# Key-feature sums as two column tiles, output weights in ten pieces, and a new instruction list

## The chip, the cores and the metric

The kernel runs on one core of a Trainium2 chip. The metric is the device time of one execution in microseconds; the median of three runs of the kernel before is 293.02 us. TensorE is the matrix engine (PE in the profile, with PEld for its weight loads), VectorE is DVE, ScalarE is ACT, GpSimd is POOL, and SyncE is SP, which here only issues DMAs.

## The reference

Two attention layers over the same input x (2048 tokens, 640 features, 32 heads of 20) are mixed by a gate per token. Cut to what matters:

```python
g = sigmoid((x * gate_w).sum(-1, keepdims=True))
# layer A: linear attention with softmax features
q, k, v = split(x @ wqkv)                       # 32 heads of 20
phi(t) = concat[softmax(t @ w_phi), softmax(-(t @ w_phi))]
kv  = sum over tokens of phi(k)^T v             # per head 40 x 20
z   = sum over tokens of phi(k)
a   = (phi(q) @ kv) / (phi(q) @ z + 1e-6) @ wo_A
# layer B: four segments of 512 tokens
p   = softmax(q k^T * scale + causal mask)      # inside a segment
mem = (pq @ M) / (pq @ z + 1e-6)                # memory of earlier segments
b   = (sig(beta) * mem + (1 - sig(beta)) * p v) @ wo_B;  M += pk^T v;  z += sum pk
out = g * a + (1 - g) * b
```

## The kernel before, in words

All matmul inputs are bf16 and sums are f32 in PSUM. Tokens are cut into 16 chunks of 128, and the 640 features into five chunks of 128. The program is one long list of words, `ORDER`. Each word is a step of a kind of work, such as `X0`, with a number behind it for the PSUM bank, or `a` where ACT and not DVE takes the copy out of PSUM. The words are run in order, and each engine keeps its instructions in that order, so the list alone decides what stands behind what on every engine. The kinds that matter here:

- `T`: x of the first 512 tokens turned on TensorE (4 x 5 transposes). `L`: the other three quarters of x, by a transposing DMA on SP. `F` and `W`: the feature matrix w_phi multiplied into the key and query weights; `F` needs the transposed key weights, which a DMA brings.
- `k`, `v`, `q`: keys, values and queries of layer B (5 matmuls each into a bank; `k1`, `v1`, `q1` the copies; `k2`, `q2` the DMAs on SP that lay keys and queries out for the scores). `K`, `Y`: key and query features of layer B.
- `A`: key features of layer A for a token chunk. `A0` is 10 matmuls, `A1` and `A2` two exps on ACT, `A3` to `A5` the sum, the reciprocal and the product on DVE, which goes to `phk`. `B`: the values `vA`, and the gate's sum.
- `S` and `s`: the sums z of the features. `X`: the sums kv. Ten `X0` (five chunks of features, two signs) have 16 matmuls each, one for every token chunk, and accumulate in one bank; `X1` is the masked copy to `KV` on DVE.
- `P`: attention scores. `P0` writes four banks (`st_ps`, from the fourth on a single buffer) with four row tiles of 32 rows, `P1` is one exp of 128 x 2048 on ACT, `P3` the mask on POOL. There are 80 such steps. `U`: scores times values on four column tiles of 32 columns (`uv_ps`), `U1` the copy to `uT`, `U2` a transposing DMA, `U3` to `U5` the division. `V`: the same for the last four heads' groups without tiles.
- `f`: query features of layer A (exps `f1`, `f2`). `d`: their denominators, `d0` 40 small matmuls and `d1` to `d6` a chain on DVE. `n`: numerators, `n0` and `n1` three matmuls each, `n2` and `n3` the scaling on DVE (which needs `d6`), `n4` the addition on POOL.
- `M`: the memory of layer B. `R`: the end of layer A's buffers; `R0` also loads the output weights `WoA` and `WoB` by two DMAs of 800 KB on SP. `l`: transposing DMAs of the finished rows. `o`: output projections, `o0` 10 matmuls. `t`, `b`, `p`, `a`, `e`, `z`, `h`: the same for the last 512 tokens, in parts.

In `products` (the word `X0`) features `c * 128` to `c * 128 + 127` belong to seven or eight heads, `lo` to `hi`; so each matmul has 128 stationary columns and (hi - lo) x 20 = 140 or 160 moving ones, and the mask `hm` keeps of the result only the blocks in which feature and value are of the same head.

Of the kernel before, what the change touches and what calls it, by code (L numbers as in the profile page):

```python
# [15 lines left out]
def kernel(  # L16
# [367 lines left out]
    def products(n, step, at, ev):  # L384
        t = item("X", n)
        c, sgn = divmod(n, 2)
        lo, hi = min(w[1] for w in ROWS if w[0] == c), max(w[2] for w in ROWS if w[0] == c)
        if step == 0:
            t.ps = bank([P, hi - lo, DH], "kv_ps", at)
            for sc in range(NCH):  # L390
                ten.matmul(t.ps, lhsT=phk[:, sc, c * P:(c + 1) * P, sgn],
                           rhs=vA[:, sc, lo * DH:hi * DH],
                           start=(sc == 0), stop=(sc == NCH - 1))
        else:
            vec.tensor_tensor(out=KV[:, c, sgn, lo - 6 * c:hi - 6 * c], in0=t.ps,
                              in1=hm[:, c, lo - 6 * c:hi - 6 * c, None].to_broadcast([P, hi - lo, DH]),
                              op=ALU.mult)
# [4 lines left out]
    def second_half(n, step, at, ev):  # L402
# [8 lines left out]
        wO = ctx.enter_context(tc.tile_pool(name="wO", bufs=1))  # L411
        lt.WoA = wO.tile([P, KC, D], BF16, name="WoA")
        lt.WoB = wO.tile([P, KC, D], BF16, name="WoB")
        syn.dma_start(out=lt.WoA, in_=rows5(A_wo))
        syn.dma_start(out=lt.WoB, in_=rows5(B_wo))

    def reorder(n, step, at, ev):
        c = 2 * n + step
# [398 lines left out]
    def tail_out(j, step, at, ev):  # L817
# [5 lines left out]
        else:  # L823
# [2 lines left out]

    STEPS = dict(w=lambda n, step, at, ev: warm_up(4, 2), T=turned, A=key, B=value, F=fold("F", WkA, WkT), W=fold("W", WqA, WqT), I=masks,
                 J=beta_gate, G=token_gate, O=both_gates, S=sums, s=blocks, X=products, Z=clear, R=second_half,
                 r=reorder, L=load_x, D=load_q, k=keys, K=key_features, v=values, q=queries, f=features,
                 d=weights, n=numerators, Y=query_features, P=scores, V=attended, U=attended_cols, M=memory, l=rows,  # L830
                 o=outputs, t=tail_A, b=tail_B, h=tail_out,
                 p=tail_first, a=tail_mid, e=tail_next, z=tail_last)
# [3 lines left out]


    ORDER = (
# [60 lines left out]

    done = {}  # L900
    for word in "".join(ORDER).split():
        i = done.get(word[:2], 0)
        done[word[:2]] = i + 1
# [33 lines left out]
```

## Time and profile before

| | |
|---|---|
| median of 3 runs | 293.02 us (291.64 to 293.09) |
| profiled execution, its own time | 292.36 us |
| its span, first to last instruction | 290.6 us |
| PE, DVE, ACT, POOL busy | 96%, 83%, 82%, 63% of the span |
| granted TensorE clock | 1.00 throughout |
| HBM | 5.61 MB read, 2.62 MB written |

The busy share of an engine is an average over stages. The profile names all instructions by one line, 117 (a helper records them), so the tiles tell them apart: `kv_ps` is X, `st_ps` P, `uv_ps` U, `num_ps` n, `o_ps` o and the tail, `k_ps` A, `v_ps` B, `proj` k and v, `fold_ps` F and W. The first transposed weights lie in the tile `phk`, which is free at that time.

### The profile page before, as it was taken

What the parts mean: (1) busy time and instruction counts of PE and PEld (TensorE: products, weight loads), DVE (VectorE), ACT (ScalarE), POOL (GpSimd) and SP (SyncE); (2) the same over time, 40 slices, a digit from 0 to 9 for tenths busy, and PEclk for the clock granted to TensorE, in tenths of its full rate; (3) what the DMA queues carried; (4) which work ended last, traced back from release to release, by engine and by line L of the source; (5) the groups of instructions that cost most, each with busy time, mean ns of one, the idle gap of its engine ahead of it and who ended that gap; (6) DMA issues with size and microseconds to landing.
All of it is one profiled execution on the core that took longest, in us unless ns stands there. A gap on an engine that the chain in (4) does not pass through costs nothing.

```text
span 290.6 us, 8207 instructions
## 1 busy us (share of the span) xinstructions
PE 278.1 (96%) x3233; PEld 176.2 (61%) x3233; DVE 239.8 (83%) x576; ACT 239.6 (82%) x260; POOL 183.8 (63%) x305
## 2 busy tenths in 40 slices
PE   8999999999999999999999999999999999898994
PEld 4676666667677546565546556556555555566673
DVE  5969999999699539999889988798898769989613
ACT  2478976998867899999999988999899998888801
POOL 8050000037346846797996899989789996998610
PEclk9999999999999999999999999999999999999999
DMA  7999960100110694546243425141736114356422
GB/s 226 252 237 215 166 142 11 36 2 20 20 20 20 203 158 89 72 86 134 39 92 72 106 58 104 39 106 36 124 72 139 26 41 111 83 122 126 106 62 90
DMA packets 79591, 28.10 MB, mean 97 GB/s; under 512 B 69952, under 2 KB 79552, under 8 KB 79552
## 3 DMA queue, kind: packets, MB, share of 16 engines
q1 hardware_dynamic: 78608, 26.84, 45.3%
q10 hardware_dynamic: 944, 0.74, 0.8%
q8 instruction: 25, 0.41, 0.6%
q14 instruction: 14, 0.11, 0.1%
HBM read 5.61 MB, written 2.62 MB: 28 GB/s over the span
## 4 chain that ended last, share of the span: by engine, by line
PE 66%; ACT 18%; DMA 5%; DVE 4%; POOL 3%; issue 3%; DVEq 0%; ACTq 0%; SPq 0%; POOLq 0%
ACT PT L117 15%; PE o_ps L117 9%; PE proj L117 8%; PE v_ps L117 8%; PE k_ps L117 8%; PE st_ps L117 7%; PE pf_ps L117 6%; PE q_ps L117 6%; PE uv_ps L117 4%; PE kv_ps L117 4%; DMA phk<-in_A_wqkv_dram 3%; PE mem_ps L117 2%; PE num_ps L117 2%; ACT ET L117 2%; PE zb_ps L117 1%
## 5 line engine op out<-in xcount | busy, mean ns | idle before, releaser
L117 ACT ACTIVATE PT<-st_ps 128x2048 bf16<-128x2048 f32 (+1 forms) x83 | 151.2, 1826 | 18.5 <-PE st_ps L117 14.0
L117 POOL TENSOR_SCALAR_AFFINE_SELECT PT<-PT 128x512 bf16<-128x512 bf16 (+2 forms) x116 | 80.5, 708 | 37.7 <-ACT PT L117 37.2
L117 PEld LDWEIGHTS <-xT 128*128 128x128 bf16 x640 | 59.5, 98 | 28.4 <-issue 5.7
L117 PE MATMUL st_ps<-qTp,kTs 32*128 32x384 bf16 (+3 forms) x512 | 31.8, 300 | 5.0 <-ACT PT L117 4.7
L117 ACT ACTIVATE Ek<-k_ps 128x640 bf16<-128x640 f32 x32 | 26.2, 893 | 6.2 <-PE k_ps L117 4.3
L117 POOL TENSOR_TENSOR Msb<-Msb,mtmp 128x84 f32<-128x84 f32 x24 | 9.3, 386 | 33.9 <-DVE mtmp L117 33.7
L117 DVE TENSOR_TENSOR t<-num_ps,dd 128x320 f32<-128x320 f32 x64 | 28.0, 481 | 2.3 <-POOL oA L117 1.3
L117 POOL TENSOR_TENSOR oA<-t,t 128x320 bf16<-128x320 f32 x32 | 29.1, 914 | 0.9 <-DVE t L117 0.7
L117 PEld LDWEIGHTS <-oT 128*128 128x128 bf16 x240 | 22.2, 98 | 10.4 <-issue 2.2
L117 PEld LDWEIGHTS <-kTs 32*128 32x128 bf16 (+1 forms) x552 | 14.8, 92 | 20.3 <-issue 16.3
L117 PE MATMUL proj<-WvB,xT 128*128 128x320 bf16 x160 | 26.2, 300 | 0.2 <-ACT vB L117 0.2
L117 PE MATMUL proj<-WkB,xT 128*128 128x320 bf16 x160 | 25.9, 300 | 0.0
L117 PE MATMUL q_ps<-xT,WqB 128*128 128x512 bf16 x100 | 24.9, 380 | 0.0
L117 PE MATMUL pf_ps<-xT,WqA 128*128 128x512 bf16 x100 | 24.9, 379 | 0.0
L117 PE MATMUL v_ps<-WvA,xT 128*128 128x320 bf16 (+1 forms) x160 | 24.5, 300 | 0.0
L117 PE MATMUL k_ps<-qTp,xT 128*128 128x320 bf16 x160 | 23.7, 299 | 0.1
L117 DVE TENSOR_REDUCE ksum<-Ek 128x64 f32<-128x1280 bf16 x16 | 23.3, 1455 | 0.0
L117 ACT ACTIVATE ET<-pf_ps 128x512 bf16<-128x512 f32 x40 | 22.0, 627 | 0.0
L117 POOL TENSOR_TENSOR oB<-td,tm 128x320 bf16<-128x320 f32 (+4 forms) x25 | 20.8, 835 | 0.4
L117 PE MATMUL o_ps<-WoA,oT 128*128 128x320 bf16 x120 | 20.3, 300 | 0.3 <-DVE tm L117 0.3
L117 PE MATMUL uv_ps<-PT,vB 128*32 128x512 bf16 (+1 forms) x448 | 20.4, 302 | 0.1
L117 PEld LDWEIGHTS <-phk 128*128 128x128 bf16 x370 | 17.6, 98 | 4.4 <-DMA phk<-in_A_x_dram 1.7
(115 smaller groups left out, 490.0 us busy)
## 6 DMA issues: line engine op xcount, KB each, us to landing
out_dram<-osb SPq DMA_DIRECT2D x12, 160.0 KB
qTp<-qd SPq DMA_DIRECT2D x8, 128.0 KB
WvB<-in_B_wv_dram SPq DMA_DIRECT2D x1, 800.0 KB
vA<-in_B_wq_dram SPq DMA_DIRECT2D x1, 800.0 KB
WvA<-in_A_wqkv_dram SPq DMA_DIRECT2D x1, 800.0 KB
WoA<-in_A_wo_dram SPq DMA_DIRECT2D x1, 800.0 KB
WoB<-in_B_wo_dram SPq DMA_DIRECT2D x1, 800.0 KB
qTp<-qd SPq DMA_DIRECT2D x8, 96.0 KB
```

Of the source, the lines that this page charges most:

```text
L117: return lambda *a, **k: kept(f(*a, **k))
```

## The change

1. In `products`, each matmul of 128 stationary columns becomes two of 64, set on the left and the right half of the array by `tile_position`. The first token chunk still multiplies all 140 or 160 value columns, so that the whole bank is written; the 15 others multiply only the 80 columns of the four heads that the 64 features touch. 160 matmuls become 320.
2. `R0` no longer loads the output weights. A new word `c0`, ten times in the list, loads one chunk of 128 rows (160 KB) each, on SP.
3. `ORDER` is written anew, with 1609 words instead of 1599 (the ten `c0`). A few copies go from one engine to the other: of `v1` three more on ACT, of `U1` and `o1` three each more on DVE; in the tail ACT takes four `h0` instead of an `h0` and an `h1`.

```diff
             for sc in range(NCH):
-                ten.matmul(t.ps, lhsT=phk[:, sc, c * P:(c + 1) * P, sgn],
-                           rhs=vA[:, sc, lo * DH:hi * DH],
-                           start=(sc == 0), stop=(sc == NCH - 1))
+                for f in range(c * P, (c + 1) * P, 64):
+                    a, b = (lo, hi) if sc == 0 else (f // DH, -(-(f + 64) // DH))
+                    r = f - c * P
+                    ten.matmul(t.ps[r:r + 64, a - lo:b - lo, :], lhsT=phk[:, sc, f:f + 64, sgn],
+                               rhs=vA[:, sc, a * DH:b * DH], start=(sc == 0), stop=(sc == NCH - 1),
+                               tile_position=(0, r), skip_group_check=True)
...
-        syn.dma_start(out=lt.WoA, in_=rows5(A_wo))
-        syn.dma_start(out=lt.WoB, in_=rows5(B_wo))
+    def load_o(n, step, at, ev):
+        W, w = ((lt.WoA, A_wo), (lt.WoB, B_wo))[n // KC]
+        syn.dma_start(out=W[:, n % KC, :], in_=rows5(w)[:, n % KC, :])
```

The places of the list that the prediction speaks of: the start, the first X blocks, the last denominators with their numerators, and the end.

```diff
-        "T00 w0 T1 T01 T02 T1 T1 T03 k00 T1 k01 k1 k02 I0 k03 k1 k00 k1 k1 K0 k01 K1 k1 K0 k02 K2 "
-        "K1 v03 k1 K2 K0 k00 k1 v1a K1 v01 k1 K2 F00 K0 L0 F01 K1 v1 v02 F1a K2 F2a v03 F1 F2 v1a "
+        "T00 w0 T1 k01 T02 k1 T03 T1 T1 k00 T01 k1 k02 T1 k03 k1 k00 K0 K1 k1 k01 K2 k1 K0 k02 I0 "
+        "v03 K1 v00 k1 k1 v1a v01 K0 K2 K1 v02 v1a v1 K2 F00 F01 v1 k2 F1a k03 F1 F2a F2 F00 k1 "
...
-        "s0 X00 s0 P1 U1 s0 U2 X02 s0 X1 s0 s0 s0 P3 P00 s0 X01 P1 X1 X03 s0 X1 s0 s0 s0 U3 P3 "
+        "B03 U3 s0 U4 M6 B12 s0 U5 B2 s0 U01 M7 B3 B4 s0 P3 P00 U1 X00 P1 s0 U2 s0 X03 s0 X1 s0 "
+        "s0 X02 X1 s0 P3 s0 P00 k01 P1 X1 k00 s0 k1 k03 s0 k1 s0 P3 K0 K1 P00 X02 P1 U01 s0 k1 U3 "
...
-        "U2 P1 Y2 o00 d1 M5 P3 P00 l0 M01 o1a M4 P1 d2 o00 M2 d3 M3 d4 U3 d5 U4 U5 o2 P00 o1a d6 "
-        "n02 P1 n13 P3 n00 n2 n3 n12 n2 M5 U03 n3 Y0 Y1 P00 n4 U1 o00 P1 M4 U2 P3 Y2 n4 n02 n13 "
+        "U03 o1 M5 d02 U1 U4 U2 U5 P00 d1 M00 P1 P3 o01 M2 M03 d2 l0 M3 o1 P3 P00 o02 M2 P1 U3 d3 "
+        "U4 M4 M3 n01 d4 M5 n10 o1 o2 P00 d5 o02 P3 P1 M4 d6 U5 n2 U03 l0 n3 o1a P3 P00 U1 n01 P1 "
...
-        "p02 V1 p11 V2 V3 P3 P00 o00 P1 M5 a0 M4 b0 o1a P3 V03 o2 V4 p00 V1 V2 V3 p01 M5 a0 b0 "
-        "p00 p13 e0 a0 e0 e0 z0 z1 z0 h0 z1 a0 h1 h0a h1 h2 h2 z0 z1 e0 h0 z0 h1 z1 h0 h2 h1a h2 ")
+        "o1 Y0 P3 P00 M4 V02 P1 M2 Y1 M5 V4 M3 o2 p01 Y2 p13 V1 P3 M4 P00 V2 P1 M00 V3 a0 M2 M5 "
+        "M3 p00 P3 b0 M4 V02 V4 p01 V1 V2 V3 a0 M5 b0 e0 e0 a0 p00 p12 z0 z1 e0 h0a h1 z0 z1 a0 "
+        "h0a h2 h1 h2 z0 z1 e0 h0a h1 z0 z1 h2 h0a h1 h2 ")
```

More of the change, by code (lines that the diff above doesn't have):

```diff
@@ L828 @@
                  J=beta_gate, G=token_gate, O=both_gates, S=sums, s=blocks, X=products, Z=clear, R=second_half,
-                 r=reorder, L=load_x, D=load_q, k=keys, K=key_features, v=values, q=queries, f=features,
+                 r=reorder, c=load_o, L=load_x, D=load_q, k=keys, K=key_features, v=values, q=queries, f=features,
                  d=weights, n=numerators, Y=query_features, P=scores, V=attended, U=attended_cols, M=memory, l=rows,
```

105 rows, old and new, of the table ORDER are left out of this document.

## The prediction

> **What bounds the kernel now.** I read the page first (span, busy shares, chain), then the stretches, the chain piece by piece, the groups by shape, the waits, and the timeline at the two places where TensorE stands still longest.
>
> ```profile
> span 290.6 us, 8207 instructions
> PE 278.1 (96%) x3233; PEld 176.2 (61%) x3233; DVE 239.8 (83%) x576; ACT 239.6 (82%) x260; POOL 183.8 (63%) x305
> PE 66%; ACT 18%; DMA 5%; DVE 4%; POOL 3%; issue 3%; DVEq 0%; ACTq 0%; SPq 0%; POOLq 0%
> ```
>
> TensorE is busy for 278.1 of 290.6 us and carries 66% of the chain. Busy is not the same as at its peak, so the next question is where it idles, and whether it runs at pace where it is busy.
>
> ```profile
> 0.00:14.00 14.00, 12.23 (x84) 7.62 (x85) 10.43 (x23) 4.64 (x7) 6.40 (x21) 1.00 0.96 234
> ...
> 66.00:81.00 15.00, 15.00 (x280) 10.48 (x283) 12.01 (x33) 12.09 (x15) 7.98 (x13) 1.00 0.09 20
> 81.00:97.00 16.00, 15.96 (x261) 12.52 (x250) 13.54 (x52) 11.94 (x7) 8.29 (x15) 1.00 0.14 28
> ...
> 140.00:155.00 15.00, 15.00 (x185) 7.90 (x184) 12.88 (x39) 14.98 (x18) 14.36 (x27) 1.00 0.33 68
> ...
> 245.00:260.00 15.00, 13.11 (x162) 8.17 (x160) 13.61 (x35) 12.47 (x11) 14.03 (x20) 1.00 0.43 97
> 260.00:275.00 15.00, 13.36 (x232) 9.61 (x231) 12.60 (x33) 12.93 (x11) 12.25 (x19) 1.00 0.56 126
> 275.00:291.00 16.00, 11.84 (x120) 8.58 (x118) 4.55 (x11) 2.46 (x4) 1.76 (x3) 1.00 0.22 69
> ```
>
> The columns are length, then PE, PEld, DVE, ACT and POOL busy, the granted clock, DMA share and GB/s. The clock is 1.00 throughout. TensorE idles 1.8 us in the first stretch, 1.9 and 1.6 us in 245 to 275, and 4.2 us at the end; in 81 to 97, where the sums that the change touches stand, it has 0.04 us to spare, with ACT at 11.9 and DVE at 13.5 of 16. There a shorter TensorE block is a shorter kernel. In 140 to 155 ACT is full too (14.98 of 15).
>
> ```profile
> 49.03 2.72 PE k_ps L117 x20
> 51.74 1.08 PE q_ps L117 x5
> 67.86 0.98 PE zb_ps L117 x40
> 81.35 2.05 PE kv_ps L117 x32
> 86.37 1.11 PE kv_ps L117 x16
> 96.27 1.19 PE q_ps L117 x5
> 97.46 1.08 PE pf_ps L117 x5
> 278.14 8.17 PE o_ps L117 x60
> ```
>
> These chain pieces (start, length) give the pace. 20 matmuls of 320 columns in 2.72 us are 136 ns each, 5 of 512 in 1.08 us are 216 ns: 0.417 ns a column plus 2.7 ns. A matmul of 4 columns (zb_ps) still takes 0.98 us / 40 = 24.5 ns, so that is a floor for one weight load with one matmul. And 5 of 512 take 1.19 instead of 1.08 us next to a tiled block: changing between the whole array and tiles costs about 0.1 us (the same 0.1 shows in 1.11 us for 16 of kv_ps).
>
> **The sums X as two column tiles.** Ten blocks of 16 matmuls now.
>
> ```profile
> L117 PE MATMUL kv_ps<-vA,phk 128*128 128x140 bf16 x128 | 8.6, 224 | 0.0
> L117 PE MATMUL kv_ps<-vA,phk 128*128 128x160 bf16 x32 | 2.6, 233 | 0.0
> L117 PE MATMUL uv_ps<-PT,vB 128*32 128x128 bf16 x112 | 6.4, 219 | 0.0
> ```
>
> At the pace, 128 of 140 columns at 61 ns and 32 of 160 at 69 ns are 10.0 us (two blocks as one chain piece: 2.05 us, with a tile change in it). After, each block is one pair at full width (61 ns) and 15 pairs of 80 columns on two halves of the array. What a pair costs no row shows. Its lower bound is one 80-column stream, 0.417 x 80 + 2.7 = 36 ns, if both halves stream at once: ten blocks are then 6.0 us, a gain of 4.0. That tiles do stream at once is shown by the attention sums on four column tiles:
>
> ```profile
> 80.62 0.73 PE L117 MATMUL uv_ps<-PT,vB 128*32 128x512 bf16 x16
> 81.01 0.11 PEld L117 LDWEIGHTS <-vB 128*32 128x32 bf16 x4
> 81.28 1.94 PEld L117 LDWEIGHTS <-phk 128*128 128x128 bf16 x32 [0.16 <-issue]
> ```
>
> Sixteen matmuls of 512, 384, 256 and 128 columns would take 2.2 us in turn, and took 0.73; four weight loads lie inside 0.11 us, hardly longer than the 96 to 98 ns of one. But there each load hides under a stream of at least 107 ns; here it has 33 ns. The upper bound is two loads and two matmuls in turn at the cost of the attention loads' 0.11 us, so about 100 ns a pair and 122 for the first: 16.2 us, a loss of 6.2. I take 50 ns, twice the 24.5 ns floor of a load with its matmul, the nearest row: ten blocks of 61 + 15 x 50 = 811 ns, 8.1 us, **a gain of 1.9 us**. The gain is gone at 63 ns a pair.
>
> The Trainium skill speaks against the change: its page TensorEngine Tiling (Restrictions and Gotchas) says that column tiling turns Fast Weight Load off, and the page "TensorE: Matmul & The Clock Gate" (LDWEIGHTS) gives a load as columns / 1.2 ns. By that a 64-column load is an estimated 53 ns, and with the loads of both halves side by side the gain would be 1.4 us instead of 1.9. No run here shows a 64-column load.
>
> Tile changes: counted in the two programs' TensorE order there are 194 before and 193 after, because the new list sets nearly every X block beside a P or U block, which is tiled anyway. So this costs nothing. The 160 more loads and 160 more matmuls are also more instructions to fetch; TensorE shows no idle time in 81 to 97 that a fetch would explain, so I take nothing.
>
> **The output weights in ten pieces.**
>
> ```profile
> 96.25 0.47 SPq L117 DMA_DIRECT2D WoA<-in_A_wo_dram  x1
> 96.77 0.51 SPq L117 DMA_DIRECT2D WoB<-in_B_wo_dram  x1
> SPq L117 <- DVE uT L117: 49.6, 17, 5.4
> L117 PE MATMUL o_ps<-WoA,oT x120: 296/299/310, 135.5 to 274.8; 128*128 128x320 bf16 x120
> ```
>
> Two issues of 0.5 us become ten, some 5 us of SP's time; SP waits 49.6 us for uT alone. What stands behind a piece (the q rows into qTp, the transposes of keys and of uT) goes out 0.5 us later, and the smaller burst behind 97 us frees the DMA engines for them. The first reader, o_ps, ran at 135.5, nearly 39 us behind the load. In the new list it stands 14 us of TensorE work later than now, and 6.8 us of TensorE work behind the last piece; a piece of 160 KB has that long. Zero either way; if a piece came late, one o_ps block (1.36 us) at most would wait, once.
>
> **The list.** Three places in it can be priced.
>
> ```profile
> 4.51 9.18 DMA phk<-in_A_wqkv_dram
> 13.73 0.81 PE L117 MATMUL fold_ps<-phk 128*128 128x140 bf16 x12 [0.51 <-DMA phk<-in_A_wqkv_dram]
> PE st_ps L117 <- ACT PT L117: 4.7, 16, 0.6
> 242.57 1.75 DVE L117 RECIPROCAL rs<-dn_ps 128x256 f32<-128x256 f32 x1
> 246.03 0.65 PE L117 MATMUL num_ps<-KV,ET 128*128 128x140 bf16 x9
> 247.85 0.32 PE L117 MATMUL num_ps<-KV,ET 128*128 128x80 bf16 x3 [1.17 <-DVE t L117]
> 244.21 1.64 issue
> ```
>
> First, the start. F00 waits 0.51 us for the transposed key weights, which land at 13.69. The old list has ten projections ahead of it, the new one eleven, and the first of them stands between the transposes T, where TensorE waits for x. One projection is 0.68 us: the 0.51 us go. What is late next is the landing itself, which nothing moves. The next quarter of x is issued one key transpose later on SP (1.2 us) while its first reader A0 comes 1.9 us of TensorE work earlier: this may take back a few tenths.
>
> Second, the last numerators. At 246.7 num_ps waits 1.17 us for DVE, which is still in the chain that starts with the reciprocal at 242.57 (d1 to d6). The old list puts n00 right behind n02 and n13, and two banks are all that it has. The new one puts P00, o02, U03 and P00 between the first pair and the next: 0.4 + 1.36 + 0.7 + 0.4 = 2.9 us of other work. **The 1.17 us go.** In the same place POOL stood 1.64 us on "issue", which looks like its instruction fetch. Where the fetches fall in the new list no row of before can tell, so I count no gain.
>
> Third, P waits for ACT: 4.7 us in 16 places, since st_ps has one buffer and an exp of it takes 1.89 us. A cycle of exp and scores is some 2.45 us. Adding up, between each P00 and the next, the TensorE work of the list at the paces above, and summing what lacks to 2.45 us, gives 9.4 us in the old list and 9.2 in the new one: no change. The new list has five U0 with only 1.7 to 2.0 us of TensorE work behind the exp that feeds them (the old one two); allowance for those 0.5 us. And at the end 8.6 us instead of 10.1 stand between the last scores and the first z0, whose chain (exp 1.9, mask 1.2, V 1.4, M5 0.5, transpose about 3) is as long: allowance 0.3 us.
>
> Sum: -1.9 - 0.5 - 1.2 + 0.5 + 0.3 = **-2.8 us**. The profiled execution took 292.36 us with its span of 290.6, so its span should fall to 287.8 and its time to 289.6. The median of the three runs is 293.02, 0.66 above the profiled one: **290.2 us**.
>
> **Rivals.**
> 1. *The halves stream at full pace* (36 ns a pair). For it: uv_ps above streams at pace. Against: its loads are shorter and have more cover. Gain 4.0 instead of 1.9: 288.1 us. The Trainium skill's packing model (page "TensorE: Matmul & The Clock Gate", Part 3: Packing small matmuls) would have a pair take one matmul and some 4 ns; an estimated 40 ns, near this rival.
> 2. *The gain is given back.* For it: ACT is full in 140 to 155, and the whole list is new, with cover that I summed by TensorE alone. 1.5 to 4 us of new waits of the kind seen at 246: 291.7 to 294.2, about 293.
> 3. *Slower: the loads of the two halves go in turn.* Price 100 ns a pair, 6.2 us more where the forecast has 1.9 less: 298.3 us; it turns the sign from about 80 ns on. For it: X runs where TensorE has no slack. Against: four loads in 0.11 us.
> 4. *Slower: a late feeder on SP or POOL in the new list*. If the U0 blocks of short cover wait for the masks (1.2 us each) in stage after stage, 5 us come together: 295.2 us. For it: POOL at 14.0 of 15 in 245 to 260. Against: the old list has such places and U0 does not show among TensorE's longest waits.
>
> **How the numbers follow.** 0.5% is 1.5 us, about what a measurement of this kernel can tell from no change; so faster means below 291.55 and slower above 294.5. Forecast 0.42, its own range 288.8 to 291.5; rival 1 0.12; rival 2 0.24; rival 3 0.08; rival 4 0.14. Faster is the forecast with rival 1, 0.54; same is rival 2, 0.24; slower 0.22. The range leaves out rival 3, the upper half of rival 4 and what is faster still than rival 1, together about 0.17: 287.6 to 295.4.
>
> **What would show it.** kv_ps after: 320 matmuls, tile 128*64, and a lone block's first and last start 0.8 us apart (0.57 for rival 1, 1.6 for rival 3). fold_ps without its 0.5 us for the DMA, num_ps without its 1.17 us for DVE. PE's waits for PT still 4 to 6 us, and idle time in 245 to 275 down from 3.5 to about 2.3 us. The forecast is wrong if kv_ps costs over 63 ns a pair, or if PE's idle time outside the first and last stretch grows by over 2 us.

## The result, and the profile after

| | before | after |
|---|---|---|
| median | 293.05 us (291.64 to 293.4, 4 runs) | 287.57 us (287.12 to 287.99, 4 runs) |
| ratio to before | 1 | 0.9837, 95% interval 0.9807 to 0.9867 |
| span of the profiled execution | 290.6 us | 285.6 us |

The change makes the kernel 1.6% faster by the ratio (4.8 us), 5.5 us by the medians and 5.0 us by the spans. The forecast was 290.2 us. It had the right side, but it fell 2.6 us short: the median lies at the very edge of its range (287.6 to 295.4 us; the ratio times the old median, 288.2 us, lies inside), close to where its first rival stood (288.1 us).

Page of the kernel after: its span, the engines' busy time, and the chain's shares by engine.

```profile
span 285.6 us, 8511 instructions
PE 272.6 (95%) x3371; PEld 173.4 (61%) x3393; DVE 237.2 (83%) x577; ACT 239.0 (84%) x259; POOL 183.0 (64%) x305
PE 67%; ACT 17%; DVE 6%; POOL 5%; issue 2%; DMA 1%; DVEq 0%; ACTq 0%
```

TensorE is busy 5.5 us less (278.1 before), DVE 2.6 and ACT 0.6 us. The 5.5 can't be taken at its word: 3371 matmul records stand beside 3393 loads, so 22 matmuls (of `q_ps` and `pf_ps`, 216 ns each) are missing from this trace and count as idle. Sums over the whole trace below therefore go by starts, not by busy time. The DMA share of the chain went from 5% to 1%.

Stretches of the kernel after (length, then PE, PEld, DVE, ACT and POOL busy, clock, DMA share, GB/s):

```profile
0.00:14.00 14.00, 12.28 (x87) 8.00 (x88) 9.85 (x21) 4.44 (x7) 6.38 (x21) 1.00 0.94 250
66.00:81.00 15.00, 14.85 (x328) 10.59 (x328) 12.32 (x43) 11.71 (x10) 6.77 (x14) 1.00 0.11 24
81.00:97.00 16.00, 15.66 (x339) 9.78 (x341) 13.63 (x50) 12.79 (x10) 10.20 (x17) 1.00 0.25 57
245.00:260.00 15.00, 14.58 (x202) 9.99 (x194) 13.74 (x35) 12.67 (x10) 14.77 (x22) 1.00 0.56 113
260.00:275.00 15.00, 13.63 (x228) 9.89 (x225) 12.31 (x33) 10.92 (x8) 10.50 (x16) 1.00 0.49 103
```

In 81 to 97 TensorE seems to idle 0.34 us where it idled 0.04; two missing records are 0.1 of that, and the rest stands before three P. In 245 to 275 it idles 1.8 us at most, where it idled 3.5.

The tile `kv_ps` of the kernel after (durations as lowest/median/highest ns, first and last start), then its blocks in TensorE's timeline (start, length in us), and its weight loads among the groups by shape (busy us, mean ns):

```profile
L117 PE MATMUL kv_ps<-vA,phk x320: 197/202/258, 78.9 to 92.4; 128*64 128x80 bf16 x150, 128*64 128x140 bf16 x8, 128*64 128x160 bf16 x2
```

```profile
78.91 1.99 PE L117 MATMUL kv_ps<-vA,phk 128*64 128x140 bf16 x96
83.82 0.80 PE L117 MATMUL kv_ps<-vA,phk 128*64 128x140 bf16 x32
```

```profile
L117 PEld LDWEIGHTS <-phk 128*64 128x64 bf16 x320 | 6.4, 111 | 1.5 <-issue 1.5
```

The duration of one matmul, about 200 ns, is not its price, since the next ones start long before it ends. The price is the distance of starts. A lone block is 0.80 us long including the last matmul's 0.20, so its starts spread over 0.60 us. Less the first pair at full width (61 ns), 15 pairs in 0.54 us are **36 ns each**. Ten blocks are 6.0 us, where they were 10.0.

The longest waits of TensorE, kernel after (us, times, longest):

```profile
PE st_ps L117 <- ACT PT L117: 4.7, 16, 0.6
PE warm_ps L117 <- DVE vA L117: 1.1, 1, 1.1
PE proj L117 <- DVE xT L117: 0.4, 1, 0.4
PE q_ps L117 <- issue: 0.3, 2, 0.2
```

The wait of `num_ps` for DVE (1.17 us) and that of `fold_ps` for a DMA (0.51 us) are gone. The waits of P for the exps stand as they did, 4.7 us in 16 places.

### The profile page after: what moved, and what is told of

It is laid out like the page before. It is cut to its first block, busy times and chain, and to the rows that moved or that the text cites. A ratio compares the mean times of both kernels' runs of the same rounds, so it can differ in the third digit from the quotient of the medians.

```text
span 285.6 us, 8511 instructions
## 1 busy us (share of the span) xinstructions
PE 272.6 (95%) x3371; PEld 173.4 (61%) x3393; DVE 237.2 (83%) x577; ACT 239.0 (84%) x259; POOL 183.0 (64%) x305
## 4 chain that ended last, share of the span: by engine, by line
PE 67%; ACT 17%; DVE 6%; POOL 5%; issue 2%; DMA 1%; DVEq 0%; ACTq 0%
ACT PT L117 15%; PE proj L117 10%; PE o_ps L117 10%; PE v_ps L117 8%; PE k_ps L117 8%; PE st_ps L117 7%; PE pf_ps L117 5%; PE q_ps L117 5%; PE uv_ps L117 4%; POOL PT L117 2%; PE num_ps L117 2%; PE mem_ps L117 2%; POOL oA L117 2%; DMA WkB<-in_B_wk_dram 1%; PE zb_ps L117 1%
## 5 line engine op out<-in xcount | busy, mean ns | idle before, releaser
L117 POOL TENSOR_SCALAR_AFFINE_SELECT PT<-PT 128x512 bf16<-128x512 bf16 (+2 forms) x116 | 78.9, 694 | 26.5 <-ACT PT L117 26.2
L117 POOL MEMSET qTp<- 128x4096 bf16 x1 | 3.5, 3512 | 39.3 <-ACT vA L117 39.3
L117 PE MATMUL pf_ps<-xT,WqA 128*128 128x512 bf16 x91 | 24.3, 380 | 0.7 <-DVE uq L117 0.2
L117 PE MATMUL q_ps<-xT,WqB 128*128 128x512 bf16 x87 | 23.7, 380 | 0.9 <-issue 0.3
L117 DVE CAST uT<-uv_ps 128x512 bf16<-128x512 f32 x28 | 18.8, 670 | 2.4 <-PE uv_ps L117 2.2
```

The source lines that it names most:

```text
L117: return lambda *a, **k: kept(f(*a, **k))
```

## The experiments

The kernel before was run beside each group of four. Ratios below are to those runs, whose medians were 291.79 us (first four experiments) and 292.4 us (last four). Spans are of single profiled executions. All executions of one kernel lie 0.9 us (the kernel after) to 3.0 us (the ten pieces in one place) apart, and those of the kernel before some 2.2 us, so a difference of about a microsecond between two spans means something only where the traces show its place.

**The list without the tiles.** The kernel after, with one 128-column matmul for each token chunk again.

```diff
-                for f in range(c * P, (c + 1) * P, 64):
-                    ...
+                ten.matmul(t.ps, lhsT=phk[:, sc, c * P:(c + 1) * P, sgn],
+                           rhs=vA[:, sc, lo * DH:hi * DH], ...)
```

> The changed kernel with its new list and the ten loads, but X as 160 matmuls of 128 columns again. Theory (the two column tiles bring four of the five us, since TensorE sets the time there): TensorE has 4.0 us more streams in X and two tile changes less (0.2 us), so the span goes from 285.6 to about 289.4 us and the ratio to the kernel before is about 0.996. Rival (the new list brings the gain by the waits it removes, the tiles are hidden): the span stays within 0.7 us of 285.6, ratio about 0.984 to 0.986.

Measured: 294.3 us, ratio 1.0078 (1.0051 to 1.0104), span 292.3 us. Without the tiles the new list is slower than the old one, more than either expectation allowed. Undoing the tiles costs 6.7 us of span, of which the blocks themselves explain 3.8 to 4.0: the exps of this kernel run 3.3 us behind those of the kernel after at the end of the sums, 4.9 us behind the step shown next and 6.6 us at 255 us. The largest piece of the rest stands 50 us behind the sums. Timeline of this kernel around 141 to 147 us, idle time before an instruction and what ended it in brackets:

```profile
141.16 1.50 SPq L117 DMA_TRANSPOSE uN<-uT  x1
145.78 0.25 DVE L117 RECIPROCAL rden<-uN 128x16 f32<-128x16 bf16 x1 [3.10 <-DMA uN<-uT]
146.63 0.84 PE L117 MATMUL proj<-WvB,xT 128*128 128x320 bf16 x5 [1.45 <-DVE uT L117]
```

The same step in the kernel after:

```profile
137.39 1.21 SPq L117 DMA_TRANSPOSE uN<-uT  x1
140.34 0.25 DVE L117 RECIPROCAL rden<-uN 128x16 f32<-128x16 bf16 x1 [1.00 <-DMA uN<-uT]
```

The transposing DMA of `uT` took some 4.6 us from issue to its reader instead of 2.9; DVE stood behind it, the copy of the next `uT` stood behind DVE, and TensorE waited 1.45 us for the bank. Shifted by some 4 us, the same list meets its DMAs in another order. This is one execution, so what delayed that one transpose is not settled, and the later pieces were not traced back.

**The tiles without the list.** The kernel before, with only the tiles.

```diff
+                for f in range(c * P, (c + 1) * P, 64):
+                    a, b = (lo, hi) if sc == 0 else (f // DH, -(-(f + 64) // DH))
+                    ... (the two half-array matmuls of the change)
```

> The kernel before with its own list, and only X as two column tiles. Theory: 3.8 us less (4.0 of streams, less two more tile changes at 0.1 us), span about 286.8 us, ratio about 0.987. Rival (the gain is the list's): span 290 to 291, ratio 0.998 to 1.001. A second rival (the list of before cannot use an earlier end of X, because exps on ACT pace what follows): half of it, span 288.5 to 289, ratio about 0.993.

Measured: 291.08 us, ratio 0.9977 (0.9956 to 0.9997), span 289.2 us. By its ratio the time is nearest to the first rival, by which the gain is the list's, but the mechanism is that of the second: the blocks are as short as in the kernel after, and the gain does not arrive. TensorE's timeline of this kernel:

```profile
80.53 1.39 PE L117 MATMUL kv_ps<-vA,phk 128*64 128x140 bf16 x64
82.31 0.40 PE L117 MATMUL st_ps<-qTp,kTs 32*128 32x256 bf16 x8 [0.39 <-ACT PT L117]
82.64 1.40 PE L117 MATMUL kv_ps<-vA,phk 128*64 128x140 bf16 x64
84.68 0.40 PE L117 MATMUL st_ps<-qTp,kTs 32*128 32x512 bf16 x4 [0.65 <-ACT PT L117]
...
87.47 1.40 PE L117 MATMUL kv_ps<-vA,phk 128*64 128x160 bf16 x64
89.57 0.40 PE L117 MATMUL st_ps<-qTp,kTs 32*128 32x512 bf16 x4 [0.71 <-ACT PT L117]
```

Behind each pair of X blocks stands a P, whose bank is free only when ACT's exp of the step before has read it. Two blocks at 1.40 us no longer cover the exp. TensorE's waits for PT, 4.7 us in 16 places before, are in this kernel:

```profile
PE st_ps L117 <- ACT PT L117: 7.6, 21, 0.7
```

2.9 us more, in five more places, and the span fell by 1.4 us. Of these 1.4 us, 0.8 lie in the first 45 us, where the two programs are the same; from there on the tiles gain 0.6. One piece of the 0.8 is the wait of `fold_ps` for its weights, 0.51 us in the trace before, which this execution does not have:

```profile
13.26 0.81 PE L117 MATMUL fold_ps<-phk 128*128 128x140 bf16 x12
```

The four kernels make a square of ratios, with the spans beside them:

| | old list | new list |
|---|---|---|
| X untiled | 1 (290.6 us) | 1.0078 (292.3 us) |
| X on two column tiles | 0.9977 (289.2 us) | 0.9837 (285.6 us) |

By the ratios, which go by all executions, the list alone loses 2.3 us, the tiles alone gain 0.7, both together gain 4.8 (1.7, 1.4 and 5.0 by the spans). The new list sets other TensorE work (keys, queries and query features) between the P steps of that stretch: in the kernel after, the timeline of 78 to 93 us shows no P with idle time before it that it puts down to the exp.

**The output weights as two loads.** The kernel after, with the two 800 KB loads at the first two `c0`.

```diff
+        if n in (0, 1):
+            W, w = ((lt.WoA, A_wo), (lt.WoB, B_wo))[n]
+            syn.dma_start(out=W, in_=rows5(w))
```

> The changed kernel, but with the output weights loaded by two DMAs of 800 KB at the first two of the ten places instead of ten of 160 KB. Theory (the pieces cost and bring nothing): span 285.6 within 0.5 us, ratio 0.982 to 0.986. Rival (the one burst holds up the q rows and key transposes behind it, and the pieces brought part of the gain): 1 to 2 us longer, ratio about 0.989, with TensorE waits for scores in 95 to 125 us.

Measured: 289.37 us, ratio 0.9903 (0.9873 to 0.9933), span 287.0 us, 1.4 us above the kernel after. TensorE and DVE in this kernel's timeline:

```profile
108.97 0.25 DVE L117 RECIPROCAL rden<-uN 128x16 f32<-128x16 bf16 x1 [2.47 <-DMA uN<-uT]
109.14 0.63 DVE L117 CAST uT<-uv_ps 128x512 bf16<-128x512 f32 x1
109.82 1.14 PE L117 MATMUL dn_ps<-HZ,ET 128*128 128x16 bf16 x40 [1.40 <-DVE uT L117]
```

In the kernel after, the same three have no idle time in brackets:

```profile
106.42 0.24 DVE L117 RECIPROCAL rden<-uN 128x16 f32<-128x16 bf16 x1
106.69 0.69 DVE L117 CAST uT<-uv_ps 128x512 bf16<-128x512 f32 x1
108.27 1.15 PE L117 MATMUL dn_ps<-HZ,ET 128*128 128x16 bf16 x40
```

The transpose of `uT` comes late behind the big transfers, and the wait reaches TensorE at `dn_ps`, over DVE: 1.40 us, which is the whole difference of the spans. Up to this place the exps of the two kernels run together to within 0.3 us, and behind it 1.3 to 1.6 us apart. The transpose went out at 102.70 us, 0.65 later than in the kernel after, and took 6.25 us from issue to reader:

```profile
102.70 6.25 DMA uN<-uT
```

The expectation's rival had the size (1 to 2 us), but the wait at another place: it looked for waits of the scores. The lowest of the six executions, 286.0 us, lies among those of the kernel after (285.4 to 286.3).

**The ten pieces in one place.** The kernel after, with all ten 160 KB loads at the first `c0`.

```diff
+        if n == 0:
+            for i in range(2 * KC): ...   # issue all ten
```

> The changed kernel with the ten loads of 160 KB all issued at the first of their places, one behind the other. Theory A (what counts is that they lie between the other transfers): as with two loads of 800 KB, 1 to 2 us more than the changed kernel, ratio 0.988 to 0.992, and a wait of dn_ps for the transposed uN near 108 us. Theory B (the size of a transfer counts): as the changed kernel, ratio 0.982 to 0.986.

Measured: 289.15 us, ratio 0.9883 (0.9847 to 0.9918), span 286.5 us, 0.9 above the kernel after. The same step waits, only less:

```profile
108.53 0.26 DVE L117 RECIPROCAL rden<-uN 128x16 f32<-128x16 bf16 x1 [1.83 <-DMA uN<-uT]
109.38 1.15 PE L117 MATMUL dn_ps<-HZ,ET 128*128 128x16 bf16 x40 [0.76 <-DVE uT L117]
```

```profile
105.20 3.31 DMA uN<-uT
```

Here the transpose itself is short, but it goes out only at 105.20 us, 3.2 later than in the kernel after: ten issues in a row stand ahead on SP. So in these traces, with the tiles and the new list, the place between the other transfers counts, about 1 us. The ratio alone does not show it, since its interval overlaps that of the kernel after (0.9807 to 0.9867). Whether the size of a piece counts beside it is not settled: this kernel and the one before differ by 0.5 us of span, and their ratios' intervals overlap.

**Half-array matmuls at full width.** The kernel after, with the same tiles and number of instructions, but all 140 or 160 columns in every one.

```diff
-                    a, b = (lo, hi) if sc == 0 else (f // DH, -(-(f + 64) // DH))
+                    a, b = lo, hi
```

> The changed kernel with its tiles, tile changes and number of instructions, but every pair at the full 140 or 160 columns (61 or 69 ns instead of 36). Theory (the streams of X lie on the path): 10 x 15 pairs x 25 ns = 3.8 us more, ratio 0.9837 + 0.013 = about 0.997. If the list passes later waits on as it did without tiles: up to 6 us more, ratio 1.000 to 1.006. Rival (X has cover, its tiles matter by the lower number of tile changes alone): under 1 us more.

Measured: 290.63 us, ratio 0.9929 (0.9903 to 0.9954), span 288.6 us, 3.0 above the kernel after.

```profile
78.73 3.11 PE L117 MATMUL kv_ps<-vA,phk 128*64 128x140 bf16 x96
84.58 1.17 PE L117 MATMUL kv_ps<-vA,phk 128*64 128x140 bf16 x32
```

A lone block's starts spread over 0.94 us, with 61 ns from pair to pair: the pace of one 140-column stream. Two halves stream at once, at either width, and the gain comes from the fewer columns. The streaming of the ten blocks grew by 4.0 us (the expectation's 3.8 left out that two blocks have 160 columns) and the span by 3.0. Counted from the starts, TensorE's waits in 75 to 97 us fell from 1.04 us (after) to 0.40, which is most of the difference: in the kernel after, some P stand a little behind the exp, and with longer blocks they don't.

**Narrow moving side.** The kernel after with 15 of 16 pairs at 20 columns; most of the sums are left out, so that only its pace is read.

```diff
-                    a, b = (lo, hi) if sc == 0 else (f // DH, -(-(f + 64) // DH))
+                    a, b = (lo, hi) if sc == 0 else (f // DH, f // DH + 1)
```

> The changed kernel, but the 15 pairs of each X block multiply only the 20 columns of one head (most of the sums is left out). It prices a pair without its stream. Theory (a pair costs its longest stream, and the loads of 64 columns hide): a pair falls from 36 ns to the floor of one round, 25 ns, and not below. Rival, the prediction's price (each matmul with its load has a floor of 24.5 ns, so a pair 50 ns): already the 36 ns speak against it; a pair would stay at 36 ns if loads or issue set it.

Measured, in one run: 287.37 us, span 285.7 us, as the kernel after (285.6).

```profile
83.89 0.40 PE L117 MATMUL st_ps<-qTp,kTs 32*128 32x512 bf16 x4
84.21 0.73 PE L117 MATMUL kv_ps<-vA,phk 128*64 128x140 bf16 x32
...
88.24 0.71 PE L117 MATMUL kv_ps<-vA,phk 128*64 128x140 bf16 x32
89.17 0.40 PE L117 MATMUL st_ps<-qTp,kTs 32*128 32x512 bf16 x4 [0.22 <-ACT PT L117]
```

The median distance of two pairs is 32 ns, so this, and not 25, is what two loads with their two matmuls cost at least. It lies just under the 36 ns of 80 columns, so the stream still sets the pace in the kernel after. The ten blocks are 0.6 us shorter, which brings nothing in this one execution: P waits for the exp instead, as in the last row.

**Four column tiles.** The kernel after, with X on four tiles of 32 columns.

```diff
-                for f in range(c * P, (c + 1) * P, 64):
+                for f in range(c * P, (c + 1) * P, 32):
```

> The changed kernel with X on four column tiles of 32 stationary columns, 40 or 60 moving columns each (the first token chunk at full width). Theory (a round costs the longest stream of its tiles, as 36 ns for 80 columns did): 0.417 x 60 + 2.7 = 28 ns a round, ten blocks 4.8 instead of 6.0 us, and three tile changes less (U has the same tiles), together 1.5 us less: span about 284.1, ratio about 0.979. Rival (a floor by load and matmul, 24.5 ns for each of the four, or the issue of eight instructions): 50 to 100 ns a round, 8 to 16 us in X, span 288 to 295, ratio 0.99 to 1.01.

Measured: 294.47 us, ratio 1.0095 (1.006 to 1.013), span 294.1 us. Rows of this kernel's timeline, then its stretch 81 to 97:

```profile
84.45 0.71 PE L117 MATMUL kv_ps<-vA,phk 128*32 128x140 bf16 x64
...
87.46 0.76 PE L117 MATMUL kv_ps<-vA,phk 128*32 128x60 bf16 x69 [1.26 <-issue]
...
94.92 0.34 PE L117 MATMUL kv_ps<-vA,phk 128*32 128x60 bf16 x22 [2.09 <-issue]
```

```profile
81.00:97.00 16.00, 11.57 (x528) 7.64 (x525) 10.33 (x39) 8.90 (x8) 6.71 (x11) 0.94 0.19 23
```

The time lies in the range of the expectation's rival, but not by the rival's price: an undisturbed block is 0.71 us instead of 0.80, so a round of four tiles is about 31 ns, near the 28 of the theory and far from the rival's 50. But TensorE then stands for nothing that the profile shows, in the middle of X blocks, 4.3 us in three places, and it is busy for only 11.57 of 16 us. A block is 128 instructions in half a microsecond. In the same stretch five instruction fetches of 16 KB ran, about a microsecond each (three in the kernel after, in 78 to 93). Each of the three stands ends 1.3 to 1.5 us after the last packet of such a fetch. That TensorE ran out of instructions fits these rows; that the fetch is what it waited for is inferred, since the waits name no releaser.

Behind the last and longest stand, the granted clock is halved for 3.4 us, which is why the stretch above has 0.94:

```profile
95.20:98.60 3.40, 3.40 (x99) 1.78 (x84) 2.13 (x11) 1.67 (x1) 0.00 (x0) 0.50 0.11 23
```

At half clock TensorE does in 3.4 us what else takes 1.7, so this adds up to 1.7 us to the 4.3. It is not the cause of the stands, which come before it.

**The last numerators moved.** The kernel before, with n00 and n12 moved behind M5 and U03.

```diff
-        "n02 P1 n13 P3 n00 n2 n3 n12 n2 M5 U03 n3 Y0 Y1 P00 n4 U1 o00 P1 M4 U2 P3 Y2 n4 n02 n13 "
+        "n02 P1 n13 P3 n2 n3 M5 U03 n00 n12 n2 n3 Y0 Y1 P00 n4 U1 o00 P1 M4 U2 P3 Y2 n4 n02 n13 "
```

> The kernel before, only with the last segment's second pair of numerator matmuls (n00, n12) moved behind M5 and U03 in the list. Prediction's step: num_ps no longer waits 1.17 us for DVE, and the time falls by 1.2 us, ratio about 0.996. Rival (the wait is handed to the next scores, which wait for ACT and POOL, POOL having stood 1.64 us in the same place): 0 to 0.4 us, ratio 0.999 to 1.000.

Measured: 293.63 us, ratio 1.0033 (1.0013 to 1.0053), span 292.0 us. Neither expectation was met: it became slower. TensorE in this kernel's timeline, and a stretch behind it:

```profile
245.39 0.49 PE L117 MATMUL num_ps<-KV,ET 128*128 128x140 bf16 x6
247.61 0.73 PE L117 MATMUL uv_ps<-PT,vB 128*32 128x512 bf16 x16 [1.73 <-DVE t L117]
249.23 1.51 PE L117 MATMUL o_ps<-WoA,oT 128*128 128x320 bf16 x5
```

```profile
248.70:252.00 3.30, 3.30 (x21) 1.73 (x21) 2.53 (x6) 2.40 (x2) 2.55 (x5) 0.50 0.09 18
```

U03 needs bank 3, which n13 holds until DVE has scaled it, and DVE scales nothing before the chain d1 to d6 is through. So the wait went to the next user of the banks and grew to 1.73 us. Right behind it the granted clock is 0.50 for 3.4 us: five matmuls of `o_ps` take 1.51 us instead of 0.84. Across this place the execution loses 2.0 us on the trace before, and 1.3 of them lie in these 3.4 us. Seven of the twelve executions have a mean clock of 0.994, which is one such stretch (half of 3.4 us in 292); their spans are 291.9 to 292.5 us, those of the other five 291.0 to 292.4. The cause of the 1.17 us is the length of d1 to d6. The new list removes the wait because it has more TensorE work between d0 and the point where the first bank is needed: 6.65 us against 5.0, added up at the paces of the prediction.

## Why the prediction was right, and where it was wrong

**The pair's price is the term that failed.** 50 ns was taken as twice the floor of a load with its matmul on the whole array (24.5 ns); it measured 36. The rule "nearest row" chose badly: the floor belongs to one load behind another in one array, while in two halves two loads and two matmuls fit into 32 ns (the narrow pairs). The better row stood in the same part of the prediction, the attention's sums on column tiles streaming at pace. X gave 4.0 us of streams instead of 1.9, the first rival. Its 0.12 was too little for the case that the trace's only tiled sums spoke for.

The page "TensorE: Matmul & The Clock Gate" of the Trainium skill (LDWEIGHTS) gave an estimated 53 ns for a load of 64 columns, and the trace does not agree: the pair's whole price is 36 ns, and the mean record of such a load is 111 ns against 96 for 32 columns (four tiles), a difference of 15 ns where the rule has an estimated 27. Its Part 3 (Packing small matmuls), an estimated 40 ns a pair, comes near the measured 36.

**Given back or not.** The sentence "a shorter TensorE block is a shorter kernel", for 81 to 97, was read from an idle time of 0.04 us. It holds for the new list and not for the old one, where 2.9 us of the 4.0 came back as waits for exps. Zero idle time says that the wait is not there yet; how far off it is has to be read from the work between the P's. That was done for the list as a whole (9.4 against 9.2 us) and rightly forecast no change in the waits (4.7 and 4.7), but not for the tiles in the old list (and the two sums themselves are twice the 4.7 us measured). The second rival, that the gain is given back, was wrong for this kernel and right for the tiles in the old list.

**The two waits.** `fold_ps` starts at 13.85 us, 0.12 later than before but with one projection (0.68 us) more ahead of it: some 0.56 us, forecast 0.5. But that wait belongs to the one execution that was profiled: with the same start of the list, `fold_ps` began at 13.26 us in the kernel with the tiles alone and at 13.41 in that with the numerators moved, without it. So the 0.5 was read from a landing that moves between executions, and that it fits is luck. Part of it came back at once: `proj` waits 0.42 us for x and 0.24 us for `WkB`, which no term of the sum has. `num_ps` lost its 1.17 us, as forecast; the same wait stands in the kernel with the tiles alone (1.17). Idle time in 245 to 275 was forecast at 2.3 and came to 1.8 us. POOL's 1.64 us on "issue" was misread as its instruction fetch: the waits of the kernel before put the same stand down to `rden`,

```profile
POOL rden L117 <- DVE rden L117: 2.0, 2, 1.7
```

that is, to DVE, still in the same d1 to d6. It was costed at nothing, so the sum is unharmed. So is it by two other slips: the 1.11 us of 16 `kv_ps` are sixteen matmuls of 160 columns at 69 ns and show no tile change, and the third rival's 80 ns is where its loss passes the 1.5 us of the measurement, while by the forecast's own terms the gain is gone at 69.

**The allowances** of 0.5 for short U0 covers and 0.3 for the end do not show as such among TensorE's waits. Counted over the whole trace (by starts: streams at the prediction's paces with 36 ns for the new pairs, 0.093 us for each tile change, the rest being waits), streams and changes fell from 269.3 to 265.2 us and waits from 16.3 to 15.4. The waits' 0.9 is what the prediction's four terms add up to; how far each of the four was met in itself is not settled beyond the two above.

**The pieces.** Against the old program the zero can't be tested by itself. Inside the new list it was wrong: loading otherwise costs 0.9 to 1.4 us in the two traces, the lower of which the ratios do not confirm. The prediction priced SP's time and the first reader `o_ps`; what suffers is a third party, the small transpose of `uT` behind the burst, with DVE and a PSUM bank between it and TensorE. Tile changes at zero and fetches at zero fit the sum; at four tiles the fetches may have stopped being free, as inferred above.

So the difference of 2.2 us between the forecast's 2.8 and the spans' 5.0 is the pair (2.1 us), with the waits in sum as forecast. That they come out so is in part luck. The prediction adds up the tiles and the list as if each stood alone; by its terms the list alone gains 0.9 us, and it lost 2.3. No kernel run here with whole sums beats the one after.

## What to carry to other kernels

Price a packed matmul from a row in which packing already runs, and price a shortened block twice: once by its own work, and once by how much of the work behind the next wait (here the exp between two P's) it takes away. Shortening a block and spacing the waits around it are one change: here, by the ratios, the tiles alone gave -0.7 us, the list alone +2.3, and both -4.8. A bulk load that is early for its own reader can still be late for others; put it in pieces where no small latency-bound transfer is queued.

## What the runs showed of the hardware

Two column tiles run side by side at 36 ns a pair for 80 columns and 61 for 140, with a floor near 32 ns; four tiles go round in about 31 ns. At that rate, 128 instructions in half a microsecond, TensorE stood for up to 2.09 us at a time on nothing that the profile shows. A transposing DMA of one tile took 2.9 us (the kernel after), 3.3, 4.6 and 6.3 us (two loads) from issue to its reader in these traces, depending on what else was under way.

The granted clock was 0.50 for 3.4 us right behind TensorE's waits of 1.73 us (the numerators moved) and 2.09 us (four tiles), and stayed at 1.00 behind those of 1.17, 1.26, 1.40 and 1.45 us. So a wait of TensorE can cost up to 1.7 us beyond its own length. Where the limit lies, and whether it is the length of one wait that decides, was not measured.
